# A planned instruction order from forward and backward passes, the gains loaded by GpSimd's queue, and GpSimd waiting for VectorE's operations

## The chip, the cores and the metric

The kernel runs on one core of one Trainium2 chip. The metric is device time in microseconds (us), one number per execution. Executions of one kernel spread by about 1% here. The trace of before comes from a run (440.47 us, clock 1.000). A run more than 1.5% above the fastest of its kernel is called slow. The ratios below leave slow runs out; medians and ranges still contain them. Each kernel was also traced once by the hardware profiler, and a trace has its own span, about 2 us shorter than the time of that run.

The engines are TensorE (PE in the profile, with its weight loads as PEld), VectorE (DVE), ScalarE (ACT), GpSimd (POOL) and SyncE (SP). A "q" behind the name, as in SPq, marks the issue of a DMA by that engine.

## The reference

Attention with normalised q and k, then an MLP with a hard-swish. All inputs and the output are float32.

```python
# q, k, v: (8 batches, 12 heads, 448 positions, 64); g_q, g_k: (64,)
q_n, k_n = rmsnorm(q, g_q), rmsnorm(k, g_k)        # x / sqrt(mean(x*x) + 1e-6) * g
attn = softmax(q_n @ k_n.T / 8)
x = (attn @ v).transpose(0, 2, 1, 3).reshape(3584, 768)
h = x @ w_in                                       # 768 x 2048
out = (h * clip(h + 3, 0, 6) / 6) @ w_out          # 2048 x 768
```

## The kernel before

The kernel works on 48 pairs of heads, six pairs to a batch. For each pair it loads k, q and v, squares k and q (`sq`), sums the squares (`ssq`), makes the reciprocal root (`rs`), scales (`qks`), transposes k and q (`kq`), multiplies the transposed k by both gains (`kp`), and then TensorE forms the scores, ScalarE the exponentials (`e`), TensorE the values. The MLP of a batch runs on TensorE beside the attention of the next batch. Attention of batch 0 has no MLP beside it.

The first `NPE` = 10 pairs are transposed by TensorE, all others by a DMA transpose that SyncE issues. The MLP's weights come in eight loads of 768 KB (four of `w_in`, four of `w_out`), issued by GpSimd.

The program is a list of steps. Each has an engine (or a choice of DVE and POOL), a guessed duration, a time `due` and its dependencies. A planner simulates the engines once, forward, and emits the steps in the simulated order. On each engine that order is then fixed: an engine that waits for one step doesn't run the next (in the trace of the changed kernel VectorE stood 6.23 us at one step).

```python
class Plan:
    DMA_LATENCY = 1.7
    SOFT, HARD = 0.64, 0.425     # planned speed of GpSimd's loads; of other DMAs beside them
    def order(self):
        ...
        while len(done) < len(self.steps):
            # the engine that can start something first; of its ready steps the one with the least due
            ...
            if s.lock and e in ("DVE", "POOL"):
                port = s.end                      # the plan lets only one of the two hold the port
            if s.xfer:
                if e == "POOL":
                    at = max(dma_soft, s.end)
                    dma_soft = at + s.xfer / self.SOFT
                    soft.append((at, dma_soft))
                    s.end = dma_soft + self.DMA_LATENCY
                else:
                    dma_free = self.hard(soft, max(dma_free, s.end), s.xfer)
                    s.end = dma_free + self.DMA_LATENCY + s.late
        return sorted(done, key=lambda s: (s.start, s.n))
...
    def load_g():                                 # four loads on ScalarE's queue
        for a in range(2):
            nc.scalar.dma_start(out=gq_t[a * 64:(a + 1) * 64, :], in_=g_q.rearrange("(p o) -> p o", o=1))
            nc.scalar.dma_start(out=gk_t[a * 64:(a + 1) * 64, :], in_=g_k.rearrange("(p o) -> p o", o=1))
    g_load = add("ACT", 2.2, 0, load_g, after=1.5, late=3.0)
    g_make = add("DVE", 0.1, 0, ..., g_load, after=7.5)      # gp = 8 * g_q * g_k
...
    # squares: ScalarE for pairs 0 to 2, then VectorE or GpSimd; scalings likewise
    parts = [add({"DVE": 0.68, "POOL": 1.04}, 0, at - 9 * hurry, ..., lock=True, after=at - 13) ...]
...
    tr = add("SP", 1.3, at - 8, lambda: nc.sync.dma_start_transpose(       # pairs 10 to 47
        out=kq[:].rearrange("p i (t c) -> p (i t) c", c=PT),
        in_=qks[0:PT].rearrange("p i t h d -> p (i t h d)")), *sc, *war, xfer=1.3, late=1.5)
    ks = add({"DVE": 0.34, "POOL": 0.6}, 0, at - 1, lambda e: (
        nc.vector if e == "DVE" else nc.gpsimd).tensor_scalar_mul(
            kp[:, 0:S], kq[:, 0], gp[:, 0:1]), tr, g_make, one_make, *kwar, lock=True)
...
    def weights(c, at, load, kept):               # at = 7.0 + 6.3 c for w_in, 35.0 + 6.3 c for w_out
        kept[c] = add("POOL", 0.9, at, lambda: load(c), gate, xfer=4.4, after=at)
...
    with tc.manual_schedule():
        for s in plan.order():
            s.fn(s.eng)
```

Here `due` of a weight load is a constant, 7.0 to 53.9 us, and no pass changes it.

## Time and profile before

| | before |
|---|---|
| time, median of the runs made beside the changed kernel | 440.89 us (440.47 to 442.52) |
| span of the traced run | 438.6 us |
| TensorE busy | 410.6 us, 94% |
| first matmul | 11.69 us |
| mean granted TensorE clock | 1.000 |

The page of before cuts the span into 40 slices of 11 us. Each digit is tenths: first of TensorE's busy time, then of its granted clock.

```profile
PE   0588799999999999999999999999999999999995
...
PEclk9999999999999999999999999999999999999999
```

Only the first five slices and the last are below 9. The windows view of before cuts more usefully, by stage. Its columns are the window, its length, the busy us (and instructions) of PE, PEld, DVE, ACT and POOL, the mean granted clock, the DMA share and GB/s.

```profile
0.00:12.00 12.00, 0.31 (x4) 0.32 (x4) 2.29 (x5) 4.33 (x10) 3.35 (x18) 1.00 0.91 240
12.00:46.00 34.00, 26.40 (x325) 15.58 (x323) 31.63 (x55) 26.48 (x43) 28.33 (x29) 1.00 1.16 258
46.00:66.00 20.00, 17.91 (x202) 11.00 (x202) 16.66 (x28) 14.29 (x31) 18.16 (x20) 1.00 1.25 216
66.00:120.00 54.00, 53.39 (x491) 28.07 (x496) 36.86 (x58) 38.13 (x64) 39.62 (x35) 1.00 0.77 184
120.00:380.00 260.00, 258.46 (x2348) 144.74 (x2359) 139.37 (x243) 156.20 (x265) 150.69 (x130) 1.00 0.53 137
```

From 66 us on TensorE is busy 53.39 of 54 us and 258.46 of 260. Before that it is idle 11.7, 7.6 and 2.1 us. A caution on the clock: its record in this trace begins at 25.86 us, and a 9 or a 1.00 before that only means that nothing was recorded. Until then a matmul of a score took 0.55 us, after it 0.36 us, so TensorE started slow. A second way to follow TensorE is used below: take from the trace the time a matmul of each shape needs at full clock (162 ns for 384 columns, 97.5 ns for one half of a score, and so on), add these up in the order of execution, and ask when TensorE had started a given amount of such work. In before, 30 us of work had been started at 62.8 us and 60 us of work at 95.6 us.

How before starts, from the timeline (start and length in us, engine, line, operation, tiles, in brackets the idle time before it and what ended it):

```profile
4.22 0.53 ACTq L254 DMA_DIRECT2D gq_t<-in_g_q_dram  x1
...
8.38 0.47 ACTq L255 DMA_DIRECT2D gk_t<-in_g_k_dram  x1
8.89 1.67 ACT L320 ACTIVATE sq<-qk 112x512 f32<-112x512 f32 x3 [6.89 <-DMA gq_t<-in_g_q_dram]
...
11.69 0.55 PE L377 MATMUL M<-ident,qks 112*128 112x112 bf16 x4 [11.69 <-DVE qks L351]
```

ScalarE's queue holds the four loads of g behind three loads of q. Its first square starts only at 8.89 us, though k landed at 4.20 us. VectorE beside GpSimd, in the same view:

```profile
16.17 2.55 DVE L322 TENSOR_TENSOR sq<-qk 112x512 f32<-112x512 f32 x1
...
17.11 1.04 POOL L322 TENSOR_TENSOR sq<-qk 112x512 f32<-112x512 f32 x1
```

A VectorE square takes 0.68 us when nothing holds it up: one begun at 35.19 us did, and there a copy on GpSimd, begun 0.01 us after it, took 1.13 us instead of 0.62. This one took 2.55 us beside a weight load's issue (15.64 to 16.53 us), a copy (begun at 16.54 us) and this square on GpSimd, and ended half a microsecond after GpSimd's square. Over the trace up to 66 us, the squares and scalings on VectorE took 5.3 us more than 0.68 us each.

The DMA transposes of `kq`, from the view of that tile between 40 and 105 us: the time from issue to landing.

```profile
DMA to landing us min/median/max: 2.7/3.4/9.1
```

The first two of them were issued at 60.51 and 63.13 us, beside the last weight loads (landed 63.55 and 69.30), and took 9.1 and 7.7 us. The six later ones took 2.7 to 3.6 us. TensorE lost nothing by the two slow ones: nobody needed them before about 70 us, and waits for `kq` cost GpSimd and VectorE 0.4 us in all. VectorE came to the `kp` of the second one just when it had landed (70.82 us), as the timeline of before shows:

```profile
63.13 3.99 SPq L388 DMA_TRANSPOSE kq<-qks  x1
...
70.84 0.43 DVE L392 TENSOR_SCALAR kp<-kq,gp 128x448 bf16<-128x448 bf16 x1
```

### The profile page before, as it was taken

The page shows a single profiled execution, that of the slowest core. Times are in us where ns is not written, and L with a number is a line of the kernel's source. Part 1 is how long each engine was busy: PE and PEld are TensorE (multiplying, and loading weights), DVE is VectorE, ACT ScalarE, POOL GpSimd, SP SyncE. Part 2 cuts the span into 40 slices and gives each one's busy share as a digit, 9 for nine tenths or more (in the row PEclk, how much of TensorE's full clock was granted, in tenths as well). Part 3 has the DMA queues.
Part 4 walks back from the last instruction along what each step waited for, and adds up shares of the span by engine and source line. Part 5 has one row for each costly group of instructions (what it writes and reads, how often), then busy time and mean ns, then how long its engine had stood idle before and what let it go on. Part 6 is the DMA issues. An engine that isn't in the chain of part 4 may idle for free.

```text
span 438.6 us, 9205 instructions
## 1 busy us (share of the span) xinstructions
PE 410.6 (94%) x3663; PEld 229.2 (52%) x3682; DVE 246.3 (56%) x417; ACT 249.0 (57%) x425; POOL 240.2 (55%) x230
## 2 busy tenths in 40 slices
PE   0588799999999999999999999999999999999995
PEld 0355455555455565554455565554455555654563
DVE  1998887657674564456555465556564444334421
ACT  3788588657765666367664677357673665123200
POOL 3499988855757567656765657747757510000000
PEclk9999999999999999999999999999999999999999
DMA  8999999877545745674465655684465420220122
GB/s 241 247 265 261 224 214 193 216 197 192 128 121 148 189 113 136 167 214 111 133 156 157 177 135 145 159 214 109 120 161 164 97 56 12 54 81 0 37 72 73
DMA packets 102923, 64.58 MB, mean 147 GB/s; under 512 B 59744, under 2 KB 99424, under 8 KB 102880
## 3 DMA queue, kind: packets, MB, share of 16 engines
q1 hardware_dynamic: 94544, 57.01, 50.6%
q0 software_dynamic: 7296, 6.29, 9.1%
q10 hardware_dynamic: 1040, 0.69, 0.5%
q8 instruction: 29, 0.48, 0.5%
q14 instruction: 14, 0.11, 0.1%
HBM read 45.61 MB, written 11.01 MB: 129 GB/s over the span
## 4 chain that ended last, share of the span: by engine, by line
PE 80%; POOL 5%; DVE 4%; ACT 3%; issue 3%; DMA 3%; SPq 1%; POOLq 0%
PE M L558 27%; PE M L533 25%; PE S L416 9%; PE X L437 8%; PE S L558 4%; PE R L437 2%; PE S L533 2%; DVE ssq L337 1%; ACT e L421 1%; POOL qks L351 1%; PE X L558 1%; POOL sq L322 1%; POOL va L359 1%; DMA gq_t<-in_g_q_dram 1%; POOL sq L329 1%
## 5 line engine op out<-in xcount | busy, mean ns | idle before, releaser
L421 ACT ACTIVATE e<-S 112x896 bf16<-112x896 f32 x192 | 166.3, 914 | 64.1 <-PE S L416 64.0
L533 PE MATMUL M<-xT,w_in_sb 128*128 128x384 bf16 (+1 forms) x679 | 145.1, 349 | 3.7 <-DVE gT L541 2.9
L351 POOL TENSOR_TENSOR qks<-qk,rs 112x512 bf16<-112x512 f32 x87 | 90.5, 1055 | 86.6 <-ACT rs L344 84.7
L558 PE MATMUL M<-w_out_sb,gT 128*128 128x384 bf16 x736 | 131.8, 326 | 0.0
L558 PEld LDWEIGHTS <-gT 128*128 128x128 bf16 x896 | 82.9, 98 | 57.8 <-issue 7.8
L533 PEld LDWEIGHTS <-w_in_sb 128*128 128x128 bf16 x768 | 69.6, 97 | 67.4 <-issue 12.5
L541 DVE SCALAR_TENSOR_TENSOR gT<-t,M 128x384 bf16<-128x384 f32 (+1 forms) x116 | 70.6, 611 | 59.1 <-ACT t L539 58.3
L539 ACT ACTIVATE t<-M 128x384 f32<-128x384 f32 (+1 forms) x116 | 62.6, 540 | 67.0 <-PE M L533 65.5
L437 PEld LDWEIGHTS <-e 112*128 112x128 bf16 x1536 | 65.1, 99 | 31.4 <-issue 16.0
L337 DVE TENSOR_REDUCE ssq<-sq 112x16 f32<-112x1024 f32 (+1 forms) x49 | 58.4, 1193 | 23.3 <-POOL sq L329 12.2
L329 POOL TENSOR_TENSOR sq<-qk 112x1024 f32<-112x1024 f32 x36 | 68.1, 1892 | 0.0
L416 PE MATMUL S<-kq,kp 64*128 64x448 bf16 x384 | 56.6, 364 | 4.1 <-DVE kp L381 1.7
L437 PE MATMUL X<-va,e 112*128 112x65 bf16 x1152 | 58.6, 196 | 0.8 <-ACT e L421 0.6
L566 DVE COPY y<-M 128x384 f32<-128x384 f32 x46 | 25.6, 556 | 59.2 <-PE M L558 59.0
L359 POOL CAST va<-vf 112x512 bf16<-112x512 f32 x48 | 31.5, 658 | 10.4 <-DMA vf<-in_v_dram 10.1
L392 POOL TENSOR_SCALAR kp<-kq,gp 128x448 bf16<-128x448 bf16 x23 | 32.3, 1402 | 5.3 <-DMA kq<-qks 5.2
L463 DVE TENSOR_TENSOR xn<-X,rd 128x384 bf16<-128x384 f32 x48 | 26.8, 558 | 1.6
L416 PEld LDWEIGHTS <-kp 64*128 64x128 bf16 x384 | 12.2, 94 | 27.7 <-issue 18.0
L437 PE MATMUL R<-va,e 112*128 112x65 bf16 x384 | 20.4, 195 | 0.0
L377 PE MATMUL M<-ident,qks 112*128 112x112 bf16 x80 | 7.9, 242 | 13.0 <-DVE qks L351 12.4
L558 PE MATMUL S<-w_out_sb,gT 128*128 128x384 bf16 x112 | 19.5, 326 | 0.0
L462 DVE RECIPROCAL rd<-X 128x6 f32<-128x6 f32 x48 | 9.2, 192 | 15.3 <-PE X L437 15.2
(42 smaller groups left out, 156.2 us busy)
## 6 DMA issues: line engine op xcount, KB each, us to landing
qk<-in_k_dram SPq DMA_DIRECT2D x48, 224.0 KB, 3.3
vf<-in_v_dram SPq DMA_DIRECT2D x48, 224.0 KB, 3.7
qk<-in_q_dram SPq DMA_DIRECT2D x45, 224.0 KB, 3.4
w_in_sb<-in_moe_w_in_dram POOLq DMA_DIRECT2D x4, 768.0 KB, 11.3
w_out_sb<-in_moe_w_out_dram POOLq DMA_DIRECT2D x4, 768.0 KB, 11.9
out_dram<-y SPq DMA_DIRECT2D x8, 336.0 KB, 3.1
out_dram<-y SPq DMA_DIRECT2D x8, 288.0 KB, 3.4
out_dram<-y SPq DMA_DIRECT2D x8, 240.0 KB, 3.2
```

The source lines that it names most:

```text
L329: parts = [add("POOL", 1.93, at - 10, lambda: nc.gpsimd.tensor_tensor(out=sq[0:PT], in0=qk[0:PT], in1=qk[0:PT], op=MULT), *ld, *war, lock= ...
L337: red = add("DVE", 0.6 * n, at - 8 * hurry + 0.5 * i0, lambda i0=i0, i1=i1, cs=cs: nc.vector.tensor_reduce(out=ssq[0:PT, cs], in_=sq[0:PT, ...
L351: sc.append(add(on, 0, at - 6 * hurry, lambda e, i=i, rs4=rs4: engines[e].tensor_tensor(out=qks[0:PT, i].rearrange("p t h d -> p h t d"), ...
L359: vc = add({"POOL": 0.61}, 0, at - 3, lambda e: engines[e].tensor_copy(out=va[0:PT, :, :, 0:D], in_=vf[0:PT].rearrange("p h (t d) -> p h t ...
L392: nc.vector if e == "DVE" else nc.gpsimd).tensor_scalar_mul(
L416: nc.tensor.matmul(out=ps[:, a, 0:S], lhsT=kp[rows, c0:c0 + 128], rhs=kq[rows, 1, :], start=True, stop=True)
L421: x = add("ACT", 0.93, at + step * (t0 + i) / T + 0.2, lambda t=t0 + i, ps=ps: nc.scalar.activation(out=e[0:PT, t], in_=ps[0:PT, :, 0:S], ...
L437: nc.tensor.matmul(out=dst[:, a * E1:(a + 1) * E1], lhsT=e[0:PT, t, a, c0:c0 + 128], rhs=va[0:PT, a, t, :], start=(first and a == 0 and t ...
L533: nc.tensor.matmul(out=m[:, 0:n], lhsT=w_in_sb[:, kt, f * 128:(f + 1) * 128], rhs=X[:, kt, :], start=(kt == 0), stop=(kt == NKT - 1))
L539: r = add("ACT", 0.08 + n / 1200, due + span, lambda: nc.scalar.activation(out=t[:, 0:n], in_=m[:, 0:n], func=RELU, bias=0.5, scale=1.0 / ...
L541: g = add("DVE", 0.12 + n / 960, due + span, lambda: nc.vector.scalar_tensor_tensor(out=G[:, f, :], in0=t[:, 0:n], scalar=1.0, in1=m[:, 0: ...
L558: nc.tensor.matmul(out=m[:, 0:HALF], lhsT=G[:, f, i * 128:(i + 1) * 128], rhs=w_out_sb[:, f, cols], start=(f == 0), stop=(f == NFT - 1))
```

## The change

The intent is a better order. The planner simulates eight times. After each forward pass a backward pass gives every step a new `due`, the latest moment at which it could start without moving the end of the simulated program. The DMA model is new: in it three rings take turns packet by packet, with at most eight DMAs of SyncE's and ScalarE's queues outstanding. The turns are an assumption of the plan that no run here tests; for the eight see experiment 4. Guessed durations are refined. The gains are loaded by two broadcast loads on GpSimd's queue. And where the plan let a locked step of GpSimd follow one of VectorE, the program now has a wait, so that GpSimd can't start early and stretch VectorE's operation (a square took 2.55 us instead of 0.68). The code calls what the two lock their port, so these are the port waits below; what the two engines share in the hardware is not shown by any trace.

```diff
-    DMA_LATENCY = 1.7
-    SOFT, HARD = 0.64, 0.425
+class Queues:                      # the plan's model: one ring per issuing engine; a turn of all rings per packet
+    def issue(self, s, at):
+        n, size = s.xfer
+        cost = size * 4e-5 if s.eng == "POOL" and size > 64 else 0.034 + size * 1.56e-5
+    def lane(self):
+        return self.issued[-8].end if len(self.issued) >= 8 else 0.0
+    def advance(self, until):
+            turn = sum(h[2] for h in on) * (0.9 if len(on) > 1 else 1.0)
...
     def order(self):
+        for n in range(self.PASSES):
+            got = self.forward()
+            ...                                     # keep the pass that ends first
+            if n < self.PASSES - 1:
+                self.backward(got)
+    def backward(self, got):
+        ...
+            s.due = at - s.on[e]                    # the latest start
...
-    g_load = add("ACT", 2.2, 0, load_g, after=1.5, late=3.0)
+    def load_g(i):
+        t, g = ((gq_t, g_q), (gk_t, g_k))[i]
+        return nc.gpsimd.dma_start(
+            out=t[:], in_=g.rearrange("(a p o) -> a p o", a=1, o=1).to_broadcast([2, D, 1]))
+    g_load = [add("POOL", 0.9, -16, lambda i=i: load_g(i), xfer=(8, 4), after=0.7, lock=True) for i in range(2)]
     g_make = add("DVE", 0.1, 0, lambda: nc.vector.scalar_tensor_tensor(
-        out=gp[:], in0=gq_t[:], scalar=8.0, in1=gk_t[:], op0=MULT, op1=MULT), g_load, after=7.5)
+        out=gp[:], in0=gq_t[:], scalar=8.0, in1=gk_t[:], op0=MULT, op1=MULT), *g_load)
...
-            ks = add({"DVE": 0.34, "POOL": 0.6}, 0, at - 1, lambda e: (
+            ks = add({"DVE": 0.36, "POOL": 1.25}, 0, at - 1, lambda e: (
...
-        kept[c] = add("POOL", 0.9, at, lambda: load(c), gate, xfer=4.4, after=at)
+        kept[c] = add("POOL", 0.9, at, lambda: load(c), gate, xfer=(48, size), after=at, lock=True)
...
+        holder = None
         for s in plan.order():
-            s.fn(s.eng)
+            ins = s.fn(s.eng)
+            if ins is not None and s.lock and s.eng in ("DVE", "POOL"):
+                if s.eng == "POOL" and holder is not None:
+                    tc.add_manual_dep(ins.ins, holder.ins.name, mybir.DependencyInfo(
+                        mybir.DependencyClass.Sync, mybir.DependencyReason.DATA), reason="port")
+                holder = ins if s.eng == "DVE" else None
```

What the diff doesn't show is what the new order does. The work is the same. The weight loads move: in before they are issued at 8, 16, 25, 34, 39, 45, 53 and 57 us, in the changed kernel at 12, 36, 43, 44, 54, 56, 73 and 74 us. VectorE's share of the `kp` operations goes from 15 to 9.

## The prediction

> **What bounds it now.** From 66 us on, TensorE: the windows view has it busy 53.4 of 54 us (66 to 120) and 258.5 of 260 (120 to 380), and its last matmul ends 4.4 us before the span of 438.6. What can be won lies before 66 us, where TensorE is idle 12 us (first matmul at 11.7), 7.6 us (12 to 46) and 2.1 us (46 to 66). While batch 0's attention runs no MLP work fills TensorE, so each delay of ScalarE or VectorE costs span.
>
> **The start.** In the timeline ScalarE's queue issues three q loads, then four loads of g (4.22, 4.79, 7.08, 8.38 us); only then come the squares, at 8.89. The chain of waits has this too: k lands at 4.20, then 4.66 us under the name of g's load, then the squares. With g on GpSimd's queue (its weight loads take 0.89 to 1.04 us each to issue, and it has nothing urgent then) the squares should start near 4.3 us and the first transpose near 7.2: -4.5 us, all critical. Risk: VectorE now needs g before its first scaling, so a late landing (g took 3.8 to 5.0 us before) gives part back.
>
> **The port.** VectorE's operations [...] stretch when GpSimd runs: squares 0.68 us alone, 2.55, 1.52 and 1.29 beside GpSimd; scalings of q and k 0.68 alone, 0.98, 1.22, 1.53; kp 0.33 alone, up to 2.0. [...] the square begun at 16.17 ended 0.5 us after GpSimd's at 18.16. From 12 to 46 us the blocked time sums to 4.4 us of a VectorE that is 93% busy, and that one square cost TensorE 1.7 us through kq. Now GpSimd waits instead; only 24 VectorE operations take part. I expect 2 to 3 us of span from this and the better order in 12 to 46, where ScalarE (busy 26.5 of 34 us, each exp 0.91) becomes the floor. The later stretches of kp are hidden behind TensorE and win nothing.
>
> **The order.** The same work, moved: kp on VectorE 15 to 9, on GpSimd 23 to 29 (1.40 us each); weight chunks 2 to 4 issued later, which frees DMA (busy throughout the first 66 us) for q, k, v. I give it 1 us in 46 to 380, with the risk of weights or a GpSimd kp coming late.
>
> **Sum.** 4.5 + 2.5 + 1 = 8 us: 433 us, range 428.5 to 438.5. That is close to the 2% line (432.3): faster 0.42, within 2% 0.56, slower 0.02.
>
> **What would show it.** ScalarE's first square at 4.2 to 4.5 us, first matmul at 7 to 8; no VectorE square or q/k scaling over 1.1 us before 46; first MLP matmul at 38 to 40 us, not 46; TensorE idle in the 34 us after its first matmul 5 us rather than 7.6; from 66 us on the same density.
>
> **What would make it wrong.** g landing after 8 us; GpSimd, 91% busy in 46 to 66, falling behind through its waits, so that batch 1 comes late and TensorE idles at 50 to 70; TensorE staying slow at the start for as long as before (matmul pairs 0.55 us until 26 us, 0.36 later); a weight chunk late for the first MLP groups; or, on the good side, the new order closing more of the 7.6 us.

## The result, and the profile after

| | before | changed |
|---|---|---|
| median of four runs | 440.89 us | 447.83 us |
| lowest to highest | 440.47 to 442.52 | 446.94 to 455.14 (the last is a slow run) |
| ratio of the fast runs | | 1.0144, interval 1.0108 to 1.0180 |
| span of the traced run | 438.6 us | 446.3 us |
| mean granted clock | 1.000 | 0.986 |

The change costs 1.4%, inside the 2% band but on the wrong side. All ratios in this document are the mean time of one kernel's fast runs over that of the other's from the same rounds, so they aren't quite the ratio of the medians that stand beside them.

The same two lines of the changed kernel's page:

```profile
PE   0788895979999999999999999999999999999995
...
PEclk9999997989999999999999999999999999999999
```

TensorE's busy time in all hardly differs (412.4 us). A hole stands in slices 7 and 9 (67 to 78 us and 89 to 100 us), with the clock down in both. The windows view of the changed kernel:

```profile
0.00:12.00 12.00, 1.11 (x8) 0.63 (x8) 3.34 (x6) 5.46 (x11) 3.63 (x19) 1.00 0.92 220
12.00:46.00 34.00, 26.98 (x340) 16.38 (x341) 30.68 (x58) 27.70 (x49) 26.83 (x31) 1.00 0.92 222
46.00:66.00 20.00, 18.05 (x200) 10.94 (x200) 16.19 (x31) 14.59 (x27) 16.84 (x18) 1.00 1.28 213
66.00:120.00 54.00, 45.68 (x392) 23.52 (x393) 22.65 (x40) 28.75 (x49) 34.57 (x33) 0.91 1.00 189
120.00:380.00 260.00, 259.01 (x2357) 143.51 (x2370) 138.10 (x244) 159.05 (x272) 164.07 (x141) 1.00 0.56 140
```

The four other rows moved by less than a microsecond of TensorE work. In the row 66 to 120 us it fell from 53.39 to 45.68 us, at a clock of 0.91.

When TensorE had started so many us of work, in the traces (us from the span's start; last column: the last microsecond of the work):

| work started | 0 | 20 | 30 | 35 | 40 | 50 | 60 | 100 | 379 |
|---|---|---|---|---|---|---|---|---|---|
| before | 11.7 | 50.3 | 62.8 | 68.5 | 74.3 | 84.9 | 95.6 | 139.2 | 433.4 |
| changed | 10.8 | 47.2 | 59.0 | 64.8 | 77.5 | 88.8 | 104.0 | 147.6 | 440.9 |

So the changed kernel is 3.7 us ahead at 35 us of work. Between 35 and 60 us of work it takes 39.2 us where before takes 27.1. After that the distance hardly changes: 8.4 us at 60 and at 100 us of work, 7.5 us at the end. The result is a lead of 3.7 us and a loss of 12.1 us. TensorE's slow start ended 4.8 us earlier in the changed kernel (21.06 instead of 25.86 us); how much of the lead comes from that was not worked out.

The start, in the timeline of the changed kernel:

```profile
1.27 1.02 POOL L347 DMA_DIRECT2D gq_t<-in_g_q_dram  x1 [0.84 <-POOLq L756]
...
2.29 0.82 POOL L347 DMA_DIRECT2D gk_t<-in_g_k_dram  x1
...
4.63 1.15 ACT L412 ACTIVATE sq<-qk 112x512 f32<-112x512 f32 x2 [2.62 <-DMA qk<-in_k_dram]
...
9.94 0.16 DVE L363 SCALAR_TENSOR_TENSOR gp<-gq_t,gk_t 128x1 f32<-128x1 f32 x1 [3.37 <-DMA gk_t<-in_g_k_dram]
...
10.79 0.97 PE L469 MATMUL M<-ident,qks 112*128 112x112 bf16 x6 [10.79 <-DVE qks L443]
```

ScalarE's first square starts at 4.63 us, as hoped. But VectorE then stands 3.37 us until the second g load lands at 9.84 us, because the plan put `gp` in front of the first scalings. The two loads of g took 6.9 and 7.5 us from issue to landing; the kernel's own plan had them landing after 4.0 and 5.0 us from the start. The loads of k, q and v issued beside them (1.2 to 2.7 us) took 4.7 to 7.9 us, so the two tiny loads fared as their neighbours of 224 KB did. Whether the crowd or their own form (128 elements of 4 bytes) made them slow was not tested: no run changes the form alone.

The loss, in the timeline of the changed kernel:

```profile
63.22 3.14 SPq L480 DMA_TRANSPOSE kq<-qks  x1
...
72.20 0.34 DVE L484 TENSOR_SCALAR kp<-kq,gp 128x448 bf16<-128x448 bf16 x1 [6.23 <-DMA kq<-qks]
...
72.61 0.61 POOL L451 CAST va<-vf 112x512 bf16<-112x512 f32 x1 [5.01 <-DVE kp L484]
...
73.16 1.86 POOL L376 DMA_DIRECT2D w_out_sb<-in_moe_w_out_dram  x2
73.58 1.01 DVE L633 SCALAR_TENSOR_TENSOR gT<-t,M 128x384 bf16<-128x384 f32 x2
...
74.18 2.08 PE L625 MATMUL M<-xT,w_in_sb 128*128 128x384 bf16 x6 [5.31 <-DVE gT L633]
...
78.36 2.99 SPq L480 DMA_TRANSPOSE kq<-qks  x1
...
89.78 0.34 DVE L484 TENSOR_SCALAR kp<-kq,gp 128x448 bf16<-128x448 bf16 x1 [5.91 <-DMA kq<-qks]
...
92.60 0.47 PE L508 MATMUL S<-kq,kp 64*128 64x448 bf16 x2 [2.52 <-ACT e L513]
```

The transpose issued at 63.22 us landed at 72.18 us, 9.0 us later. VectorE, whose next instruction in the fixed order was the `kp` of that transpose, stood 6.23 us. GpSimd stood 5.01 us, because its next instruction had to wait for that same `kp`. TensorE's next MLP group needed a `gT` that stood behind `kp` in VectorE's order: TensorE stopped for 5.31 us. The transpose issued at 78.36 us took 11.4 us. VectorE again stood at its `kp`, for 5.91 us; the sums of squares behind it, and with them ScalarE's exponentials, came late, and TensorE stopped for 2.52 us. Before each of them a weight load had been issued that was still moving: those issued at 53.62 and 55.85 us landed at 63.28 and 71.07 us, the two issued at 73.16 us and 74.13 us landed at 83.52 and 89.34 us.

The two stops differ. For the second, before's transpose in the same place (the fourth, issued at 76.67 us) took 3.4 us: there the late weight loads made it slow. For the first, before's transpose in the same place (the second, issued at 63.13 us) took 7.7 us, nearly as long as the 9.0 us here, and weight loads were moving in both. What differs is that VectorE came to its `kp` at 65.97 us in the changed order, and in before at 70.84 us, when the data was there. The waits view of the changed kernel between 50 and 105 us (engine, tile and line, what it waited for, total us, times, longest):

```profile
DVE kp L484 <- DMA kq<-qks: 15.4, 3, 6.2
...
PE M L625 <- DVE gT L633: 6.8, 3, 5.3
...
POOL va L451 <- DVE kp L484: 5.0, 1, 5.0
```

In before the first of these lines is 0.2 us. The view of the tile `kq`, same stretch, as shown for before:

```profile
DMA to landing us min/median/max: 2.6/4.8/11.4
```

The stops also cost clock. This is the windows view of the changed kernel with windows of 3.41 us, laid so that the changes of clock fall on their edges:

```profile
68.85:72.26 3.41, 0.03 (x1) 0.00 (x0) 0.06 (x1) 0.00 (x0) 0.00 (x0) 1.00 1.26 244
72.26:75.67 3.41, 1.49 (x5) 0.69 (x5) 3.38 (x7) 1.94 (x4) 3.06 (x4) 0.50 1.16 243
75.67:79.08 3.41, 3.41 (x20) 1.49 (x19) 1.12 (x2) 2.32 (x4) 3.12 (x4) 0.50 1.14 169
79.08:82.49 3.41, 3.41 (x36) 1.93 (x35) 1.78 (x2) 1.77 (x3) 3.41 (x4) 1.00 1.37 129
89.32:92.73 3.41, 0.89 (x10) 0.43 (x7) 2.85 (x7) 1.42 (x4) 2.48 (x3) 1.00 0.68 197
92.73:96.14 3.41, 3.07 (x12) 1.17 (x10) 1.06 (x2) 2.24 (x3) 3.41 (x4) 0.50 0.99 49
96.14:99.55 3.41, 3.41 (x23) 1.75 (x22) 1.93 (x3) 0.94 (x3) 2.16 (x4) 1.00 0.87 215
```

After a window in which TensorE was idle, or busy for 0.89 us only, the granted clock is 0.50. It comes back after a window that was busy throughout, or for 3.07 of 3.41 us. The four changes, at 72.26, 79.08, 92.74 and 96.15 us, lie two, four and one such windows apart. One of the two falls came after a window that was not idle but 26% busy. TensorE worked 1.49 + 3.41 + 3.07 = 8.0 us at half speed (a matmul of 384 columns every 0.320 us instead of every 0.162) and so lost 4.0 us. With the stops, 5.31 + 2.52 + 0.34, this makes 12.2 us, which is the 12.1 us of the table. The first stop with its slow windows is 7.8 us of that, the second 4.4 us.

### The profile page after: what moved, and what is told of

It reads as the page before. It is cut to its first block, busy times and chain, and to the rows that moved or that the text cites. A ratio compares the mean times of both kernels' runs of the same rounds, so it can differ in the third digit from the quotient of the medians.

```text
span 446.3 us, 9209 instructions
## 1 busy us (share of the span) xinstructions
PE 412.4 (92%) x3663; PEld 229.2 (51%) x3682; DVE 232.5 (52%) x412; ACT 246.9 (55%) x425; POOL 245.9 (55%) x237
## 4 chain that ended last, share of the span: by engine, by line
PE 77%; DMA 3%; ACT 1%; DVE 1%; issue 0%; POOL 0%
PE M L625 26%; PE M L650 26%; PE S L508 8%; PE X L529 7%; PE S L650 4%; DMA kq<-qks 3%; PE S L625 2%; PE R L529 2%; PE X L650 1%; PE R L650 1%; PE X L625 1%; PE R L625 1%; ACT e L513 0%; DVE ssq L429 0%; DVE gT L633 0%
## 5 line engine op out<-in xcount | busy, mean ns | idle before, releaser
L513 ACT ACTIVATE e<-S 112x896 bf16<-112x896 f32 x192 | 164.5, 914 | 46.3 <-PE S L508 46.0
L625 PE MATMUL M<-xT,w_in_sb 128*128 128x384 bf16 (+1 forms) x679 | 146.7, 351 | 9.6 <-DVE gT L633 8.6
L650 PEld LDWEIGHTS <-gT 128*128 128x128 bf16 x896 | 84.4, 98 | 63.2 <-issue 12.0
L443 POOL TENSOR_TENSOR qks<-qk,rs 112x512 bf16<-112x512 f32 x86 | 88.0, 1042 | 46.8 <-ACT rs L436 31.3
L529 PEld LDWEIGHTS <-e 112*128 112x128 bf16 x1536 | 62.7, 99 | 25.0 <-issue 13.0
L484 POOL TENSOR_SCALAR kp<-kq,gp 128x448 bf16<-128x448 bf16 x29 | 40.7, 1402 | 33.4 <-DMA kq<-qks 32.3
L529 PE MATMUL X<-va,e 112*128 112x65 bf16 x1152 | 52.9, 195 | 0.1
L451 POOL CAST va<-vf 112x512 bf16<-112x512 f32 x48 | 29.2, 612 | 23.6 <-PE R L529 12.4
L435 ACT ACTIVATE rs<-ssq 112x16 f32<-112x16 f32 (+1 forms) x49 | 10.7, 218 | 24.0 <-DVE ssq L429 24.0
```

The costliest lines, as they stand in the source:

```text
L443: sc.append(add(on, 0, at - 6 * hurry, lambda e, i=i, rs4=rs4: engines[e].tensor_tensor(out=qks[0:PT, i].rearrange("p t h d -> p h t d"), ...
L451: vc = add({"POOL": 0.61}, 0, at - 3, lambda e: engines[e].tensor_copy(out=va[0:PT, :, :, 0:D], in_=vf[0:PT].rearrange("p h (t d) -> p h t ...
L513: x = add("ACT", 0.93, at + step * (t0 + i) / T + 0.2, lambda t=t0 + i, ps=ps: nc.scalar.activation(out=e[0:PT, t], in_=ps[0:PT, :, 0:S], ...
L529: nc.tensor.matmul(out=dst[:, a * E1:(a + 1) * E1], lhsT=e[0:PT, t, a, c0:c0 + 128], rhs=va[0:PT, a, t, :], start=(first and a == 0 and t ...
L625: nc.tensor.matmul(out=m[:, 0:n], lhsT=w_in_sb[:, kt, f * 128:(f + 1) * 128], rhs=X[:, kt, :], start=(kt == 0), stop=(kt == NKT - 1))
L650: nc.tensor.matmul(out=m[:, 0:HALF], lhsT=G[:, f, i * 128:(i + 1) * 128], rhs=w_out_sb[:, f, cols], start=(f == 0), stop=(f == NFT - 1))
```

## The experiments

The theory when the experiments were planned: the backward pass pushes the weight loads late, they then run beside the first DMA transposes, and these land so late that engines with a fixed order stand. Rivals: the order of `kp` between VectorE and GpSimd, the new port waits, or the place of the g loads. Single letters in the texts are names for these theories, as each text says. "Frozen order" below means that the planned order was kept and single steps were moved in it before the program was emitted. Times of before are those of the same rounds: medians of 441.25 us for experiments 1 to 4, 443.23 for 5 to 8, 441.35 for 9 to 12, 441.58 for 13 to 16, and 442.58 for the repeat of 12 and for 17. The kernels with an edit in their head have other line numbers.

**1. The weight loads alone moved forward**, in the changed kernel's frozen order.

```diff
+        for n, x in enumerate([W_in[c] for c in range(4)] + [W_out[c] for c in range(4)]):
+            if n:
+                x.start = 9.3 + 5.8 * n
```

> The changed kernel's order, with the weight loads alone moved forward in GpSimd's order (about one per 5.8 us from 9 us on; last issue near 50 instead of 74 us). Theory W (late weight loads slow the transposes that bring kq, and the engine that waits for kq stops TensorE): kq's second to fourth transposes land within 5 us of issue instead of 8.9, 3.7 and 11.4; VectorE's wait for kq from 60 to 100 us falls from 15.4 us to under 4; TensorE is idle under 2.5 us from 66 to 120 instead of 8.3; mean granted clock 1.00 instead of 0.986; time 435 to 439 us. Rival P (GpSimd's port waits are what stalls) and rival K (it is the engine chosen for kp): 445 us or more, VectorE's wait for kq over 10 us.

Measured: 447.07 us, ratio 1.0123 (1.0075 to 1.0171). A miss. The loads were issued at 12 to 50 us, but they overlapped, each took 10.6 to 17.8 us, and the last landed at 68.04 us, hardly earlier than before's 69.30. The first transpose, issued at 55.17 us, landed at 67.80 us, after 12.6 us. The waits view of this run between 50 and 105 us:

```profile
POOL kp L484 <- DMA kq<-qks: 9.4, 2, 8.6
...
DVE kp L484 <- DMA kq<-qks: 6.9, 1, 6.9
```

The second to fourth transposes did land within 3.1 us, as the theory had it, and the second stop is gone. But the first was late, now GpSimd stands for `kq` as well as VectorE, and TensorE was idle for 7.6 us from 66 to 120 us. By time alone the run fell where rivals P and K were put. What follows: moving the weights forward by some microseconds isn't enough. In before, here and in experiment 11 the last weight load lands at 66.7 to 69.3 us, and the changed order needs its first transposes before that.

**2. Four early `kp` given to GpSimd**, so that VectorE never stands for them.

```diff
+        for P in range(NPE, 18):
+            if KS[P].eng == "DVE":
+                KS[P].eng = "POOL"
```

> The changed kernel's order with the four early kp scalings from transposed kq (pairs 11 to 14), which stood on VectorE, put on GpSimd at the same places. Rival K (a blocked VectorE is what stops TensorE): VectorE's wait for kq is gone, the 5.3 us stop of TensorE at 69 us falls under 2 us, time 438 to 442. Theory W with kp needed by TensorE soon after in any case: the stops move to the score matmuls, TensorE idle over 5 us from 66 to 120, time 444 to 448.

Measured: 451.67 us, ratio 1.0236 (1.0170 to 1.0303), so not better than the change itself (1.0144; the intervals overlap), and longer than either reading had it (448 us at most). VectorE no longer waits for the transposes, but between 50 and 105 us GpSimd does (11.5 us), and VectorE then waits 20.0 us for GpSimd's squares. The engine that stands is a matter of the order; the late transposes stay (up to 10.4 us).

**3. Without the port waits.**

```diff
-                if s.eng == "POOL" and holder is not None:
+                if False:
```

> The changed kernel's order with GpSimd's explicit waits for VectorE's two-input operations left out. Theory W: the kq landings and TensorE's stop at 69 us stay, GpSimd no longer stands still with VectorE (its 7.5 and 5.0 us waits go), time 444 to 449; VectorE's early squares and scalings stretch over 1.2 us again. Rival P: TensorE's idle time from 66 to 120 us falls under 4 us, time 436 to 441.

Measured: 447.72 us, ratio 1.0142 (1.0096 to 1.0189), the same as with them. Yet the waits do what they were made for: without them VectorE's squares and scalings up to 66 us took 9.2 us more than 0.68 us each, with them 1.9 us, and 30 us of work were reached at 64.3 us instead of 59.0. Those 5.3 us are gone at 60 us of work (104.7 against 104.0), which fits a TensorE that only arrives earlier at the same late transposes.

**4. The gains by two loads on ScalarE's queue**, behind the first q, in the changed kernel's frozen order.

```diff
-        return nc.gpsimd.dma_start(
+        return nc.scalar.dma_start(
...
+        for i, x in enumerate(g_load):
+            x.eng, x.start = "ACT", 0.71 + 0.01 * i
```

> The changed kernel's order, g loaded by two DMAs on ScalarE's queue right after its first q load instead of on GpSimd's. If g's late landing (9.9 us) is what keeps the first matmul at 10.8 us: g lands by 6.5 us, first matmul at 7.5 to 8.5 us, TensorE 2 to 2.5 us ahead of the changed kernel until 60 us; time 444.5 to 446 (-2 to -3). If the later stops swallow it (they end when a DMA lands, not when the engines are ready): within 1 us of the changed kernel's 447.8.

Measured: 447.52 us, ratio 1.0140 (1.0082 to 1.0198). No gain. The first matmul came at 9.28 us instead of 10.79 (7.5 to 8.5 expected; VectorE waited for g until 8.42 us), but now the q loads were late: the second was issued at 2.89 and landed at 10.03 us. The ninth such DMA was issued at 4.46 us, just after the first k load had landed at 4.44 us. In before too the ninth was issued at 4.22 us, when the first k load had landed at 4.20; the plan in the diff counts on at most eight outstanding, and g had taken two of the places.

**5. Before's order with g on GpSimd's queue**, first on that queue.

```diff
-            nc.scalar.dma_start(out=gq_t[a * 64:(a + 1) * 64, :], in_=g_q.rearrange("(p o) -> p o", o=1))
-            ...
+            nc.gpsimd.dma_start(out=t[:], in_=g.rearrange("(a p o) -> a p o", a=1, o=1).to_broadcast([2, D, 1]))
...
+        g_load.eng, g_load.start = "POOL", -1.0
```

> One part of the change alone: the earlier kernel's order, g loaded by two DMAs on GpSimd's queue, first thing there. g should land near 9.5 us as in the changed kernel, so the multiply that makes gp (second after the first scaling of k in this order) ends near 9.8 us instead of 11.8; first matmul at 7.5 to 8.5 us instead of 11.7 (the first scaling does not wait for g here). If the front is worth anything at the end: 438 to 440 us. If it is swallowed later, when kq's transposes land together with the last weights near 69 us: 440 to 441.5, with the lead gone by 75 us.

Measured: 442.50 us beside 443.23, ratio 1.0018 (0.9966 to 1.0070). The first matmul came at 7.8 us, 3.9 us earlier than in before, but the lead was gone by 25 us of work (58.2 us, before 57.4). An early start alone brings nothing in the end here.

**6. Before's order with the weight loads at the changed kernel's places.**

```diff
+        for x, t in zip([W_in[c] for c in range(4)] + [W_out[c] for c in range(4)],
+                        (12.0, 36.4, 43.0, 43.1, 53.6, 55.9, 73.2, 74.1)):
+            x.start = t
```

> The earlier kernel's order, its weight loads alone moved back to the places that they have in the changed kernel (last issues near 73 us). Theory W2 (weight loads that run while the transposes run make these land late, and that is the loss): kq of pairs 12 to 14 lands 3 to 9 us later than before, TensorE loses 4 to 10 us between 66 and 110 us, the granted clock drops under 1.00, time 444 to 450. Rival O (it is the new order of the engines that stalls, not the weights): within 2 us of 441.

Measured: 455.26 us beside 443.23, ratio 1.0299 (1.0234 to 1.0363). The waits view of this run between 50 and 105 us:

```profile
POOL kp L392 <- DMA kq<-qks: 6.6, 1, 6.6
...
PE M L559 <- DMA w_out_sb<-in_moe_w_out_dram: 4.1, 1, 4.1
```

A transpose issued at 87.97 us landed at 100.09 us, in the instant in which the last weight load landed (100.10), so TensorE's stop of 4.1 us can't be told apart between the two. The sum is as the theory wants it, but the place isn't. Of the lag behind before, 8.1 us were there at 35 us of work (76.6 us, before 68.5). The timeline of this run shows why:

```profile
40.28 4.56 DVE L351 TENSOR_TENSOR qks<-qk,rs 112x512 bf16<-112x512 f32 x2 [0.19 <-ACT rs L344]
...
45.60 0.50 PE L477 MATMUL M<-ident,xn 128*128 128x128 bf16 x3 [3.95 <-DVE xn L464]
```

Two scalings on VectorE, 0.69 us each when alone, took 4.56 us beside GpSimd, which had issued three weight loads fewer by then and came early; another took 4.96 us at 62.90 us. These are collisions with GpSimd, with TensorE stops of 3.95 and 3.99 us. Only the last 5.7 us, between 50 and 55 us of work, belong to the stop at the last weights. This run moves the collisions too, and is no clean test.

**7. Before's order with the port waits alone.** The loop at the end of the diff, in before.

```diff
+                if s.eng == "POOL" and holder is not None:
+                    tc.add_manual_dep(ins.ins, holder.ins.name, ..., reason="port")
+                holder = ins if s.eng == "DVE" else None
```

> One part alone: the earlier kernel's order on every engine, plus GpSimd's waits for VectorE's two-input operations in the planned order (not on the weight loads). VectorE's stretched squares and scalings before 46 us go back to 0.7 us, GpSimd waits up to 4 us more in all; TensorE 1.5 to 4 us ahead by 46 us. If this reaches the end: 437 to 439.5. If the lead is swallowed by the landings near 69 us: 440 to 442.

Measured: 440.53 us, ratio 0.9963 (0.9905 to 1.0022). VectorE's stretching fell from 5.3 to 1.2 us, and the time didn't measurably move.

**8. The changed planner with 14 pairs transposed by TensorE**, so that no transpose is needed while weights move.

```diff
-    NPE = 10
+    NPE = 14
```

> The changed kernel with 14 pairs instead of 10 transposed by TensorE (everything planned anew), so that the first kq transpose by DMA comes after the weights are in. TensorE has 4 x 0.9 us more to do. Theory W2: no engine waits over 2 us for a kq landing, TensorE idle from 66 to 120 us under 3 us instead of 8.3, clock 1.00, time 439 to 443. Rival O: the stops stay in another form, 446 or more.

Measured: 450.18 us, ratio 1.0147 (1.0057 to 1.0236), a miss, and the trace fell in a slow run. The last two weight loads were issued at 61.3 and 65.8 us and landed at 80.9 and 87.3 us, and the first transpose of `kq` was issued at 88.9 us, after them. Yet TensorE was idle for 9.1 us from 66 to 120 us. Two of its stops (2.36 and 1.58 us, before 74.88 and 86.99 us) go back to GpSimd standing for loads of v, which took 11.3 and 12.4 us beside the weights (issued at 59.07 and 68.04 us). That is rival O's case, stops in another form at 446 us or more: late transposes of `kq` are not all that the weights' traffic can do. As the run is slow, its lengths are no measure.

**9. Five of the eight weight loads left out**, in the changed kernel's order. Its output is wrong, which doesn't matter for the time. The MLP uses the three loads that are left, in the same matmuls.

```diff
-                    lhsT=w_in_sb[:, kt, f * 128:(f + 1) * 128],
+                    lhsT=w_in_sb[:, kt, f % 8 * 128:(f % 8 + 1) * 128],
-                    rhs=w_out_sb[:, f, cols],
+                    rhs=w_out_sb[:, f % 8, 0:HALF],
+        if c > 1: return          # in load_w_in; c > 0 in load_w_out
```

> Wrong result on purpose: the changed kernel with the same order, but 5 of the 8 weight loads left out (the MLP matmuls use the loaded ones again; all other work and every other instruction is the same). If weight loads that run beside the transposes are the cause (W2): from 60 us on no kq transpose lands later than 5 us after issue, VectorE's wait for kq from 60 to 100 us under 3 us instead of 15.4, clock 1.00, the lead of 3.5 us over the earlier kernel at 60 us stays: 434 to 438 us. If the new order stalls for another reason (O): 444 or more.

Measured: 438.13 us, ratio 0.9939 (0.9895 to 0.9983). The changed kernel's ratio was 1.0144, so this is about 2% or 9 us less. The view of the tile `kq` in this run between 40 and 105 us:

```profile
DMA to landing us min/median/max: 2.6/3.7/5.3
```

No transpose took over 5.3 us, TensorE was busy 52.70 of 54 us between 66 and 120 us, and the clock was 0.999. The step from 35 to 60 us of work took from 65.2 to 93.5 us, 28.3 us instead of 39.2. The order, the port waits and the g loads are those of the changed kernel; only the five loads are gone, with their issues on GpSimd (0.9 us each). This settles that the weight loads' traffic is what the 9 us are paid for. The waits view of the changed kernel between 50 and 105 us puts no wait of TensorE down to the weights themselves, so it isn't their own arrival that is saved. What the run can't tell apart is the place of the loads and the place at which the order needs the transposes; experiments 1 and 11 bear on that.

**10. The same five loads left out of before.** The edit is that of experiment 9, in before:

```diff
+        if c > 1: return          # in load_w_in; c > 0 in load_w_out
```

> Wrong result on purpose: the earlier kernel with the same 5 weight loads left out. Its transposes near 60 us land within 5 us instead of 9; but its TensorE stood still little after 60 us, so W2 says 438 to 441 us, 2 to 5 us longer than the changed kernel without those loads. Rival F (the early stretch of both is bound by DMA alone): 435 or less, and equal to the changed kernel without those loads.

Measured: 444.51 us, ratio 1.0065 (1.0032 to 1.0098), above both expected ranges. So the weights' traffic did not cost before anything that comes back when it is gone. It even got slower: GpSimd ran ahead, and its squares collided with two VectorE scalings (1.4 us together when alone) in the timeline of this run:

```profile
42.63 4.17 DVE L355 TENSOR_TENSOR qks<-qk,rs 112x512 bf16<-112x512 f32 x2 [0.20 <-ACT rs L348]
...
47.55 0.50 PE L480 MATMUL M<-ident,xn 128*128 128x128 bf16 x3 [3.56 <-DVE xn L467]
```

The two scalings took 4.17 us. TensorE stopped for 3.56 us and had a mean clock of 0.85 between 46 and 66 us. As in experiment 6, before's order without port waits is at the mercy of when GpSimd comes.

**11. The changed planner with the weights' `due` pinned early**, so that the backward pass can't move them.

```diff
+        for s in got:                       # at the end of backward()
+            if s.xfer and s.xfer[0] == 48:
+                s.due = s.after - 100.0
```

> The changed kernel, planned anew, with one rule added: weight loads are not given their latest place by the backward pass but go as soon as their set time allows (planned issues 8.6 to 55 us instead of 9 to 71). W2: no landing of kq over 6 us late after 70 us, clock nearly 1.00; the first two kq (issued while the last loads run, until about 68 us) may still come late and stop TensorE once: 439 to 445 us. If moving the weights is no remedy in any order: 446 or more.

Measured: 446.35 us, ratio 1.0111 (1.0082 to 1.0140). The last weight load landed at 66.70 us, the first transpose, issued at 57.43, at 66.87 us. TensorE stopped 5.2 us. The later transposes took at most 5.0 us, as expected, but the time missed the 439 to 445 us of the theory and lies where the text says that moving the weights is no remedy. This agrees with experiment 1 in a freshly planned order: early weights take away the second stop and not the first.

**12. As 11, with 12 pairs transposed by TensorE**, g planned 4.5 us later, and transposes planned at twice the time while weights move.

```diff
-    NPE = 10
+    NPE = 12
-    g_load = [add("POOL", 0.9, -16, ..., xfer=(8, 4), after=0.7, lock=True) for i in range(2)]
+    g_load = [add("POOL", 0.9, -16, ..., xfer=(8, 4), after=0.7, lock=True, late=4.5) for i in range(2)]
...
             turn = sum(h[2] for h in on) * (0.9 if len(on) > 1 else 1.0)
+            if len(on) > 1 and ...:              # a weight load and a transpose are both on
+                turn *= 2.0
```

> As the previous one, with 12 pairs instead of 10 transposed by TensorE, g's landing planned 4.5 us later (as measured) and transposes planned at twice the cost while a weight load runs. W2: the first kq transpose by DMA is issued at 68 us or later, when the weights are in; no wait for kq over 2 us, TensorE idle from 66 to 120 us under 2.5 us, clock 1.00; TensorE has 2 x 0.5 us more to do: 437 to 441 us. If it is over 445, late transposes are not the whole cause.

Measured: 439.77 us (437.61 to 444.45, the last a slow run), ratio 0.9948 (0.9906 to 0.9990). It looked like a version that beats both, so it was repeated with more rounds:

> The run with weights pinned and 12 pairs again, for its time: ratio to the earlier kernel 0.990 to 0.999 if the first result was no luck; its spread should stay wide (438 to 444 us), because the first kq transpose by DMA lands when the weights do and TensorE stops or not by a small margin. If the ratio is 1.000 or more, no version of these beats the earlier kernel.

Measured: 440.91 us (439.05 to 443.98), ratio 0.9974 (0.9936 to 1.0011). The gain isn't confirmed. In both traces the first transpose, issued at 66 us, still met the last weight load (72.8 us) and took about 10 us, and TensorE stopped about 5 us. But both traces are of runs at the long end of the spread (444.45 us, slow, and 443.84 us); whether the stop is missing in the short runs isn't on record.

**13 and 14. As 12, with 13 and with 14 pairs.**

```diff
-    NPE = 12
+    NPE = 13      # experiment 14: 14
```

> As the run with 12 pairs, with 13: the first kq transpose by DMA is planned at 79 us, after the weights (in near 70 to 73 us). If the overlap of first transposes and weight stream is what was left: kq lands within 4 us of issue, no engine waits over 2 us for kq, TensorE idle from 66 to 120 us under 2 us, clock over 0.995, time 435 to 439 us. If something else stops TensorE near 75 us: 441 or more.

> The same with 14 pairs: no more to win from the landings, 0.5 us more TensorE work: 0 to 1 us longer than with 13 pairs, 435.5 to 440 us. If the stop near 75 us depends on other things: unlike the run with 13 pairs by over 2 us.

Measured: 440.70 us, ratio 1.0008 (0.9961 to 1.0055), and 440.81 us, ratio 0.9999 (0.9958 to 1.0041), beside 441.58. With 13 pairs the last weights landed at 69.27 us and the first transpose was issued at 77.54 us. The view of `kq` of the 13-pair run and the row of its windows view:

```profile
DMA to landing us min/median/max: 2.7/3.0/4.9
```

```profile
66.00:120.00 54.00, 53.08 (x515) 28.86 (x517) 31.90 (x60) 37.39 (x63) 41.11 (x37) 1.00 0.66 176
```

The stops are gone and the clock is 1.00 in this stretch (0.994 over the run, with 3.41 us at 0.50 from 41.25 us on). So with the transposes after the weights, a plan of this kind runs without these stops. The time that was expected, 435 to 439 us, was missed all the same: the kernel reached 35 us of work at 67.3 us instead of 64.8, so most of the lead was gone by then. Early weights and three more pairs on TensorE are the likely price; it wasn't taken apart.

**15. Before's own planner with 13 pairs.**

```diff
-    NPE = 10
+    NPE = 13
```

> Control: the earlier kernel and its own planner with 13 pairs transposed by TensorE instead of 10. Its TensorE hardly waited for kq, so 1.5 us more TensorE work and nothing won: 440.5 to 444 us. If it comes out under 439, the gain of the runs with 12 to 14 pairs is due to the pairs and not to the new planning.

Measured: 448.39 us, ratio 1.0183 (1.0127 to 1.0239). That is above the expected range: in the old planner more TensorE transposes are a loss; the clock was 0.87 between 46 and 66 us.

**16. Before's order with g on GpSimd's queue and the port waits together.** The edits of experiments 5 and 7:

```diff
+        g_load.eng, g_load.start = "POOL", -1.0
+                    tc.add_manual_dep(ins.ins, holder.ins.name, ..., reason="port")
```

> The earlier kernel's order with g on GpSimd's queue and GpSimd's port waits together (the change without its new order). Alone they gave ratios of 1.002 and 0.996. If leads made before 60 us are swallowed when kq lands near 69 us: 439.5 to 442, lead gone by 80 us. If together they reach the end: 436 to 439.

Measured: 443.08 us, ratio 1.0042 (1.0016 to 1.0068), a microsecond above the nearer expected range. It led before by 2.9 us at 20 us of work (47.4 us) and had lost that at 25 us (58.2 us, before 57.4): loads of v, k and q issued at 38.8 to 42.7 us took 13.1 to 13.7 us beside the weights, and TensorE stopped for 3.6 us.

**17. Experiment 9 without the port waits.** In the kernel of experiment 9:

```diff
-                if s.eng == "POOL" and holder is not None:
+                if False:
```

> Wrong result on purpose: the changed order with 5 of 8 weight loads left out, and GpSimd's explicit waits for VectorE left out too. If the waits are worth what they gain before 64 us (5 us there, without them): 441.5 to 444.5 us against 438.1 with them; VectorE's squares and scalings before 66 us stretched by over 6 us in all instead of under 2.5. If they are worth nothing in the end: 437.5 to 439.5.

Measured: 438.81 us beside 442.58, ratio 0.9913 (0.9885 to 0.9941). At 30 us of work the run with waits is 2.9 us ahead (59.5 against 62.4 us), and in the total the ratios don't tell the two apart. The text gave 437.5 to 439.5 us to the view that the waits bring nothing in the end, and that is where it fell. Even without the late transposes the waits' gain isn't seen in the total. VectorE's squares and scalings were stretched by 5.3 us before 66 us, with the waits by 1.8 us (over 6 and under 2.5 expected).

## Why the prediction was wrong

**The start: right in kind, mis-sized.** The square did start at 4.63 us (4.2 to 4.5 predicted), but the first matmul came at 10.79 us, not at 7.2. Of the 4.5 us 0.9 came. The risk named in the prediction, g landing after 8 us, is what happened: 9.84 us, with `gp` ahead of the scalings in VectorE's order. Its size had been read from g loads issued at 4 to 8 us (3.8 to 5.0 us in the prediction, 3.2 to 5.0 in the trace), not from loads issued in the crowd at 1 to 3 us, where the k, q and v loads of the same trace took 4.4 to 6.3 us.

**The start: wrong that all of it is critical.** "All critical" doesn't hold. Experiment 5 had the start at 7.8 us and no gain; its lead was gone at 58 us.

**The port: right about the stretching.** VectorE's stretching fell from 5.3 to 1.9 us. Up to 46 us no square was over 0.68 us; of the scalings one took 1.33 and one 1.12 us, so the predicted bound of 1.1 us was just missed. The first MLP matmul came at 39.88 us (38 to 40 predicted; 45.48 in before), and TensorE was idle for 6.5 of the 34 us after its first matmul (5 predicted; 7.6 in before). Both squares told of above show one engine held up by the other: the one begun at 16.17 us ended 0.57 us after GpSimd's work of 15.64 to 18.15 us, and at 35.19 us, where VectorE came first, GpSimd's copy was the one that took 0.5 us longer. By what rule one of the two is held up is not shown. The gain of 2 to 3 us shows as a lead at 30 us of work, 5.3 us against experiment 3, and is not to be measured in the total of any of the four pairs of kernels that differ in the waits alone (experiments 3, 7, 16 against 5, and 17).

**The order: this is the step that failed.** The prediction gave the order "1 us in 46 to 380" and argued "weight chunks 2 to 4 issued later, which frees DMA (busy throughout the first 66 us) for q, k, v", and that "from 66 us on the same density" would hold. The first half may be right: the changed kernel had its lead of 3.7 us at 65 us of the trace, though no run shows how much of it the order brought. The density did not hold: from 66 to 120 us TensorE was busy for 45.68 us instead of 53.39, at a clock of 0.91. The step that failed is that the order was taken to have no wait for `kq` in it. The changed order puts VectorE's `kp` before the transposes can land beside weight loads, and work that TensorE needs stands behind that `kp`. In the first stop this is so with loads issued at 53.62 and 55.85 us, about when before's last two were; the transpose took 9.0 us where before's took 7.7, but was wanted 4.9 us earlier. In the second stop the two loads moved to 73 and 74 us stretched a transpose to 11.4 us that took 3.4 in before. The cost was 12.1 us instead of a gain of 1. Experiment 9, which leaves weight loads out, takes 28.3 us for the stretch that cost the changed kernel 39.2. Experiments 1 and 11, with the weights early, keep a first stop of about 5 us and lose the second, and 13 has neither when the transposes begin after the weights. The prediction had named a weight chunk late for the MLP as a risk, but not what a weight chunk does to other DMAs.

**Why the planner walked into it.** It has a DMA model, and by that model there was no loss: its plan (printed by running the kernel's planner) has the transpose of the traced 63.22 us going from 64.5 to 69.0 us (4.5 us; measured 9.0), and the one of 78.36 us from 75.2 to 80.4 us (5.2 us; measured 11.4). The old, cruder model was nearer: before's plan allows its first two transposes of `kq` 8.3 and 8.9 us, and they took 9.1 and 7.7. So the finer model itself took the margin away. A backward pass makes each step as late as the model allows, so a wrong duration finds no slack left. No run was made of the changed planner with the old durations for transposes, so that this alone would have prevented the loss isn't shown. The traces show that a transpose slows down beside weight loads that another queue issued (11.4 us against 3.4 for the fourth one); how much had to be measured.

**The range.** 428.5 to 438.5 us was missed by 9 us, and "slower" had got 0.02. The time lies within 2%, which had 0.56, but for reasons that the prediction didn't hold.

**What stays open.** Why a transpose takes so long beside a weight load (11.4 us against 3.4) was not taken apart; it would need transposes of other sizes beside one load. Why the kernel of experiment 12 spreads over 437.6 to 444.5 us is open too. And other leads in batch 0 were lost too (2.9 us in experiment 16 by 25 us of work; of the 2.9 us between experiments 9 and 17 under 2 are left at 60 us of work); which wait takes them was not settled in each.

## What to carry to other kernels

A plan that starts each step as late as it can is only as good as its longest underestimated duration, because it leaves no slack. Moving only the bulk loads early did not mend that here (447.07 and 446.35 us in experiments 1 and 11); the steps that wait for the slow transfer have to be planned later as well, and even that only got back to before's time (experiments 13 and 14). A DMA on the critical path should be planned with its duration beside the bulk traffic that will run with it, as a trace shows it (9.0 and 11.4 us here, where the plan had 4.5 and 5.2), and an engine with a fixed order should not have such a DMA's consumer in front of work that others wait for. An early lead counts only if the next wait isn't for something that comes at a fixed time (the 3.9 us of experiment 5 were gone at 58.2 us): look for that wait before adding gains up.

## What the traces show of transposes, small loads and the clock

- Transposes of `kq` that mostly took 2.6 to 5 us from issue to landing took up to 12.6 us beside 768 KB loads from GpSimd's queue (9.0 and 11.4 us in the changed kernel, 12.6 us in experiment 1).
- Two tiny loads, issued at 1.27 and 2.29 us among 224 KB loads, took 6.9 and 7.5 us, as long as those (4.7 to 7.9 us). In before four loads of g, of half the size and from ScalarE's queue, took 3.2 to 5.0 us when issued at 4 to 8 us; what of the difference is due to the queue or the form isn't shown.
- In the changed kernel a gap of 2.52 us was enough to halve the clock: the window that held it was 26% busy (0.89 of 3.41 us), and the clock was 0.50 after it. A window 44% busy (1.49 of 3.41 us) didn't bring the full clock back. In the traces of before and of the changed kernel, cut into windows of 3.41 us on the grid of each clock record and read from the first rise to 428 us, the clock fell after two windows, 1% and 26% busy; all other windows at 1.00 were at least 55% busy, and the clock stayed. It came back to 1.00 after windows 100% and 90% busy.
